# A delta-rule attention feeding an exact-GELU feed-forward on one core: head's copies on ScalarE, weight decoding reordered, one weight load, one solve and one Gram product moved

## The chip, the core and the metric

The program runs on one core of a Trainium2 chip. The metric is the device time of one launch in microseconds. It has five engines with a queue each: TensorE (PE, its weight loads PEld), VectorE (DVE), ScalarE (ACT), GpSimd (POOL) and SyncE (SP), which here issues almost all DMAs.

## The reference

q, k and v are (4, 8, 768, 48): four sequences, eight heads, 768 tokens, head size 48.

```python
k_n = k / (norm(k, axis=-1) + 1e-06)
for t in range(S):
    y[:, :, t] = einsum('bhd,bhde->bhe', q[:, :, t], state)
    v_old = einsum('bhde,bhd->bhe', state, k_n[:, :, t])
    state = state + beta[:, :, t] * einsum('bhd,bhe->bhde', k_n[:, :, t], v[:, :, t] - v_old)
x = y.transpose(0, 2, 1, 3).reshape(B * S, H * D)      # (3072, 384)
h = x @ w_in                                           # w_in (384, 2048)
out = (0.5 * h * (1 + erf(h / sqrt(2)))) @ w_out       # w_out (2048, 384)
```

All is fp32. The words of `w_in` and `w_out` reach the kernel as 64-bit floating numbers, two 32-bit words each, and the kernel makes fp32 of them itself.

## The kernel before, in words

The 768 tokens are cut into 12 chunks of 64; a chunk has two units (`a` = 0, 1), each of two sequences side by side on 128 partitions. For a chunk the recurrence becomes a triangular system of its 64 tokens: Gram products of the keys (`grams`, L419, matmuls psG at L414 and copies at L425), an elimination of its diagonal 32x32 blocks on VectorE for two chunks together (L496 to L503, the transposes back at L512 and L516), and two joining products (psJ; L548 with copies L559 and L563 for the first pair of chunks, L593 later). Then come the products with the running state (`against_state`, psK L667), the right side W (`subtract`, L678 and L684, with y copied at L679), the solution U (`solve`, psU L702, copied by `solved` at L710 and L712), the reading and the change of state (`use`, psY L732, and `update`, L743), the add into the state St (`next_state`, L748), the copy of the reading into x (`read`, L756 or L758), and its transpose xT (`turn`, psX L776 or L779, copied at L780). xT is the input of the feed-forward of that chunk.

The feed-forward of chunks 0 and 1 is plain: `fc1` makes 16 groups of 128 hidden units (psH, L811: three matmuls of 256 columns, six records in the trace, then a GELU on ScalarE, at L902 for chunk 0 and at L817 for chunk 1), `fc2` multiplies them with `w_out` (psO, L829, each product two records, copied at L833). psH and psO share a tag with two buffers, so group f + 2 needs the GELU of group f. From chunk 2 on the two layers use a scheme with fewer products (L916 and L859), which needs sums of weights made beforehand (`sum_of_w_in`, `sum_of_w`).

The weights are decoded in 16 parts: parts 0 to 7 are `w_in` (each serves two groups of fc1), 8 to 15 are `w_out` (`n_in` is 8). A part n passes through `fetch` (L202, DMAs at L213, into four slots for `w_in`, into three for `w_out`), `begin` (the exponent bits, DVE, L231 or L234), `exponents` (ScalarE, L237, or L902 where it is kept in program order), `mantissas` (DVE, L251 and L253) and `signed` (DVE, L260 and L261, after which the slot is fetched anew: part n + 4, or n + 3 for `w_out`). `two_kinks(n)` (L218) picks between two ways: one activation on ScalarE and L260 on DVE, or two activations on ScalarE and no L260. In the kernel before, parts 3 to 7, 9, 10, 12 and 14 use two.

Order. The head is written by hand: everything between L1075 and L1172 keeps its program order on all five engines. After it, VectorE alone keeps the order that `emit` makes: a plan of steps with due times (L1195 and after), sorted by these, in units where the fc1 and fc2 of chunk c lie between about c + 1 and c + 2. The other engines are arranged by the framework's scheduler from the same order, save that `keep` (L901) holds an instruction of ScalarE to its place, and that `together` and `behind` chain products of TensorE. `decode_in` (L278) holds the due times of parts 3 to 7. `load` (L100) fetches keys and queries of a chunk, `load_v` its values, `load_blocks` (L138) the keys or queries of later chunks in sixteen small DMAs. `late` (L1177) closes the pools of the head and opens others in their place.

The part written by hand ends with: decoding of parts 0 to 2, `solve`, `use`, `read`, `turn` and `update` of chunk 0, and its `next_state`. Chunk 1 follows in the plan, between the groups of the first fc1.

Of the kernel before, what the change touches and what calls it, by code (L numbers as in the profile page):

```python
# [19 lines left out]
def kernel(  # L20
# [28 lines left out]
    nc = tc.nc  # L49
# [6 lines left out]
    NA = B // 2  # L56
# [38 lines left out]
    tiles = {}  # L95
# [7 lines left out]
    for c in range(NC):  # L103
        for a in range(NA):
            u = tiles[c, a] = Unit()
# [48 lines left out]
    first = [tiles[c, a] for c in range(2) for a in range(NA)]  # L154
# [38 lines left out]
    n_in = len(w_parts)  # L193
# [23 lines left out]

    def two_kinks(n):  # L218

        return 2 < n < n_in or n > n_in and n % 2 == 0 or n == n_in + 1  # L220

    def high(e, dt):

# [2 lines left out]
    def begin(n):  # L226
        e = su.tile([128, WG], U32, tag="w_e", name="w_e")
        raw = w_raw.pop(n)
        halves[n] = w_parts[n][0].rearrange("q m n -> q (m n)"), raw[:, :, 0], raw[:, :, 1], e
        if two_kinks(n):  # L230
            nc.vector.tensor_scalar(e.bitcast(I32), raw[:, :, 1].bitcast(I32), 20, -1,  # L231
                                    op0=ALU.arith_shift_right, op1=ALU.bitwise_and)
        else:
            nc.vector.tensor_scalar(e, raw[:, :, 1], 20, 0x7FF, op0=ALU.logical_shift_right,  # L234
                                    op1=ALU.bitwise_and)

    def exponents(n, put=lambda fn, *args, **kw: fn(*args, **kw)):  # L237
        e = halves[n][3]
        if two_kinks(n):
            f = e.bitcast(F32)  # L240
            put(nc.scalar.activation, f, e.bitcast(I32), ACT.Prelu, bias=lim[:, 2:3], scale=1.0,
                alpha=FLAT)
            put(nc.scalar.activation, high(e, I16), f, ACT.Prelu, bias=lim[:, 3:4], scale=128.0,
                alpha=1.0 / FLAT)
        else:
            put(nc.scalar.activation, e, e, ACT.Relu, bias=lim[:, 0:1], scale=float(2 ** 23))

    def mantissas(n):
        dst, lo, hi, e = halves[n]
        bits = dst.bitcast(U32)  # L250
        nc.vector.tensor_scalar(bits, hi, 0xFFFFF, 0x100000, op0=ALU.bitwise_and,  # L251
                                op1=ALU.bitwise_or)
        nc.vector.scalar_tensor_tensor(dst, lo, 2.0 ** -32, bits, ALU.mult, ALU.add)  # L253

    def signed(n):

        dst, lo, hi, e = halves.pop(n)
        scale = high(e, BF16) if two_kinks(n) else e.bitcast(F32)
        if not two_kinks(n):
            nc.vector.scalar_tensor_tensor(e, hi, 0x80000000, e, ALU.bitwise_and, ALU.bitwise_or)  # L260
        nc.vector.scalar_tensor_tensor(dst, dst, 2.0 ** -20, scale, ALU.mult, ALU.mult)  # L261
        after = n + (NS if n < n_in else len(slots))
        if (after < n_in) == (n < n_in):
            fetch(after)
# [426 lines left out]
    def solve(us, copies=(nc.scalar.copy, nc.scalar.copy)):  # L691
        psU = dn("psU")
        for u in us:
            zf = Zf[(u.c // 2) % 2]
            if u.c == 0 and u.a:
                psU = dn("psU")
            u.psU = quarters(psU[:, :, u.a * NP * D:(u.a + 1) * NP * D])
            for k in range(NP // 2):
                for r in range(2):
                    for p, s in SIDES:  # L700
                        h = 4 * k + 2 * s + r
                        nc.tensor.matmul(u.psU[HALF[p ^ s], s, k, r, :],  # L702
                                         lhsT=zf[HALF[p], u.t * H + h, :],
                                         rhs=u.W[HALF[p], h, :], start=True, stop=True)
        for u, copy in zip(us, copies):
            solved(u, copy)
# [10 lines left out]
    def use(us):  # L717

        for u in us:
            if u.c == 0 and u.a == 0:  # L720
                u.psY = [ps.tile([128, NP * D], F32, tag="mlp", name="psY").rearrange(
                    "q (k r d) -> q k r d", r=2, d=D) for s in range(2)]
            else:
                psY = dn("psY")
                both = quarters(psY[:, :, 0:NP * D])
                u.psY = [both[:, s] for s in range(2)]
                u.psS = psY[:, :, NP * D:2 * NP * D].rearrange("q p (j d) -> q p j d", d=D)
            for k in range(NP // 2):
                for r in range(2):
                    for p, s in SIDES:  # L730
                        h = 4 * k + 2 * s + r
                        nc.tensor.matmul(u.psY[s][HALF[p ^ s], k, r, :], lhsT=u.P[HALF[p], h, :],  # L732
                                         rhs=u.U[HALF[p], h, :], start=True, stop=True)
            if u.c > 0:
                update(u)

    def update(u):
        if u.c == 0 and u.a == 0:
            u.psS = dn("psS")[:, :, 0:NP * D].rearrange("q p (j d) -> q p j d", d=D)
        if u.c < NC - 1:  # L740
            for j in range(NP):
                for r, p in QUADS:
                    nc.tensor.matmul(u.psS[HALF[r], p ^ r, j, :], lhsT=u.Kp[HALF[p], 2 * j + r, :],  # L743
                                     rhs=u.U[HALF[p], 2 * j + r, :], start=True, stop=True)

    def next_state(u):
        if u.c < NC - 1:
            nc.vector.tensor_tensor(St[:, u.a], St[:, u.a], u.psS, op=ALU.add)  # L748

    def read(u, copy=nc.scalar.copy):  # L750
        u.x = wk.tile([128, H, D], F32, tag="x", name="x")
        both = slice(0, 128)
        for to, at_, s in ((both, both, 0), (HALF[0], HALF[1], 1), (HALF[1], HALF[0], 1)):
            dst, src = pairs(u.x[to], s), u.psY[s][at_]
            if u.c < 2:
                copy(dst, src)  # L756
            else:
                nc.vector.tensor_tensor(dst, src, pairs(u.y[at_], s), op=ALU.add)  # L758
# [7 lines left out]
    def turn(u):  # L766
        if u.a == 0:
            xTs[u.c] = wk.tile([128, NM, NA * 128], F32, tag="xT", name="xT")
        xT = xTs[u.c]
        psX = sq("psX", NM, 128)  # L770
        for m in range(NM):
            cols = slice(m * 128, (m + 1) * 128)
            if u.c == 1:

                for i, part in enumerate((u.x, u.y)):
                    nc.tensor.matmul(psX[:, m, :], lhsT=part.rearrange("q h d -> q (h d)")[:, cols],  # L776
                                     rhs=ident, start=i == 0, stop=i == 1)
            else:
                nc.tensor.transpose(psX[:, m, :], u.x.rearrange("q h d -> q (h d)")[:, cols], ident)  # L779
        nc.scalar.copy(xT[:, :, u.a * 128:(u.a + 1) * 128], psX)  # L780
# [273 lines left out]
    def at(first, last, steps):  # L1054

        total, done, timed = sum(s[0] for s in steps), 0.0, []
        for w, *step in steps:
            timed.append((first + (last - first) * (done + 0.5 * w) / total, step))
            done += w
        return timed  # L1060
# [90 lines left out]
    exponents(0)  # L1151
    mantissas(0)
    begin(1)
    solve(first[:NA], (nc.scalar.copy, nc.vector.tensor_copy))
    exponents(1)
    use(first[:NA])
    read(first[0])
    read(first[1], nc.vector.tensor_copy)
    signed(0)
    mantissas(1)  # L1160
    for u in first[:NA]:
        turn(u)
        update(u)
    signed(1)
    begin(2)
    exponents(2)
    mantissas(2)
    signed(2)
    begin(3)
    for u in first[:NA]:  # L1170
        next_state(u)
    by_hand.close()  # L1172
    free.append(True)
    tc.no_sync_barrier()
# [13 lines left out]
    def state_at(c, *times, first=(), second=()):  # L1188

        steps = state_steps(c, first, second)  # L1190
        if len(times) > len(steps):
# [3 lines left out]
    plan = [at(c + 1 + 0.25 * (c == 1), c + 2 + 0.25 * (c == 0), ffn_steps(c)) for c in range(NC)]  # L1195
    plan += [decode_in(), at(1.365, 1.9, decode_steps(n_in, NW)), at(1.91, 1.911, [(1.0, late)])]
    rows1, join1 = eliminate_steps(1), join_steps(1)
    plan += [at(0.98, 0.985, [(1.0, load, 3)]),
             [(t, (join, 0, range(NA, 2 * NA), level)) for level, t in enumerate((1.085, 1.16))],
]  # L1200
    sums = [(1.0, sum_of_squares, tiles[3, a], h) for a in range(NA) for h in range(H)]
    plan += [at(1.48, 1.8, sums), at(1.81, 1.811, [(1.0, fn, c) for c in (2, 3) for fn in (norms, prep)]), at(1.9, 1.905, [(1.0, finish_both)]), at(2.725, 2.726, [(1.0, queries, third)]),
             at(1.31, 1.311, [(1.0, together, (against_state, first[NA:]))]),
             at(1.361, 1.362, [(1.0, subtract, first[NA:])]),
             at(1.4, 1.401, [(1.0, together, (solve, first[NA:], ()))]),
             at(1.43, 1.431, [(1.0, solved, first[NA], kept_copy)]),
             at(1.455, 1.456, [(1.0, solved, first[NA + 1], kept_copy)]),
             state_at(1, None, None, 1.5, 1.56, 1.58),
# [7 lines left out]
             at(2.7, 2.701, [(1.0, together, join1[1]), (0.0, copy_out, "join", 4)]),  # L1216
             at(2.75, 2.751, [(1.0, together, join1[2]), (0.0, copy_out, "join", 4)]),
             state_at(2, None, 2.772, 2.851, 2.906, 2.922),
             at(2.728, 2.729, [(1.0, norms, 4), (1.0, prep, 4)]), at(2.8, 2.9, [(1.0, grams, [tiles[4, a] for a in range(NA)])])]
    plan += [at(0.995, 1.0, [(1.0, load_v, 2)]), at(2.727, 2.728, [(1.0, sum_of_w, 1, 2)]), at(2.96, 2.961, [(1.0, last_sum_of_w)]), at(3.07, 3.071, [(1.0, sum_of_w, 4)])]  # L1220
    plan += [at(c + 0.958, c + 0.959, [(1.0, mix_x, c)]) for c in range(2, NC)]
    plan += [at(c - 0.4, c - 0.3, v_steps(c)) for c in range(4, NC)]
    plan += [at(2.08, 2.44, [(1.0, scale_head, tiles[c, a], h)
# [110 lines left out]
```

## Time and profile before

| | |
|---|---|
| median of three runs | 646.69 us (646.2 to 648.64) |
| profiled execution | 647.7 us, span 645.9 us |
| TensorE matmuls, busy | 619.9 us (96% of the span), 9702 records |
| TensorE weight loads, busy | 574.0 us |
| VectorE, busy | 496.5 us, 1016 instructions |
| ScalarE, busy | 259.2 us, 581 instructions |
| GpSimd, busy | 62.2 us |
| mean granted TensorE clock | 0.987 |

How to read it: the profile is one execution, and times in it count from its first instruction. An engine's busy share is a mean over stages with different limits; a stage is read from the timeline of its window, where a bracket gives the idle time ahead of an instruction and what ended it. The ends of matmuls are modelled, so two that follow each other overlap on paper; the distance of their starts is the better measure. In the names, `w_e` is the exponent tile of a part, `w_raw` and `w_out_sb` as a source hold undecoded words, `G` holds hidden units, or Gram blocks where its source is psG.

### The profile page before, as it was taken

The numbers are of one execution on the slowest core, as the hardware profiler recorded it, in microseconds if no ns is written. First come the engines' busy times: TensorE is split into PE (matmuls) and PEld (weight loads), VectorE is DVE, ScalarE is ACT, GpSimd is POOL, SyncE is SP. The second block draws the span as 40 slices with busy tenths as digits, with TensorE's granted clock in tenths as the row PEclk, the third lists the DMA queues.
The fourth block names the chain that finished last, engine by engine and source line by source line (L and its number), as shares of the span: only waits on it lengthen the run. The fifth ranks groups of instructions, "written<-read, shape, count | busy, mean of one in ns | idle before, by whom it ended". The sixth has DMA issues, their size and how long they took to land.

```text
span 645.9 us, 22148 instructions
## 1 busy us (share of the span) xinstructions
PE 619.9 (96%) x9702; PEld 574.0 (89%) x9702; DVE 496.5 (77%) x1016; ACT 259.2 (40%) x581; POOL 62.2 (10%) x58
## 2 busy tenths in 40 slices
PE   6769989999999999999999999999999999999997
PEld 5657767776699999999999999999999999999997
DVE  6998789997899997999677999677999564354342
ACT  3574777624452157033157132156132253132230
POOL 4043001100221004001004001004001000000000
PEclk9986999999999999999999999999999999999999
DMA  9794755202433235321325312402212400100101
GB/s 131 174 275 131 155 140 166 37 14 45 80 57 49 56 41 92 52 35 31 68 32 89 59 26 34 73 16 40 50 24 36 69 3 3 25 2 2 26 3 24
DMA packets 158433, 39.79 MB, mean 62 GB/s; under 512 B 150016, under 2 KB 153216, under 8 KB 158336
## 3 DMA queue, kind: packets, MB, share of 16 engines
q1 hardware_dynamic: 155344, 36.94, 29.4%
q10 hardware_dynamic: 2992, 1.43, 1.0%
q8 instruction: 76, 1.25, 0.8%
q14 instruction: 21, 0.17, 0.1%
HBM read 33.62 MB, written 4.72 MB: 59 GB/s over the span
## 4 chain that ended last, share of the span: by engine, by line
PE 83%; DVE 7%; ACT 3%; DMA 3%; issue 2%; SPq 2%; ACTq 0%; DVEq 0%
PE psX L859 12%; PE psY L916 11%; PE psX L916 8%; PE psY L859 8%; PE psV L916 5%; PE psZ L916 5%; PE psO L829 5%; PE psZ L859 4%; PE psG L414 4%; PE psV L859 4%; PE psH L811 3%; PE psK L667 3%; PE psJ L593 2%; PE psY L732 2%; PE psU L702 2%
## 5 line engine op out<-in xcount | busy, mean ns | idle before, releaser
L916 PE MATMUL psX<-xT,w_in_sb 128*128 128x128 f32 x480 | 64.6, 278 | 0.3 <-DVE p L1013 0.2
L503 DVE TENSOR_TENSOR Nu<-Nu,tmp 128x58 f32<-128x58 f32 (+13 forms) x168 | 59.1, 352 | 5.8
L501 DVE TENSOR_TENSOR tmp<-Nu 128x58 f32<-128x58 f32 (+13 forms) x168 | 58.2, 346 | 4.4
L916 PEld LDWEIGHTS psX<-xT,w_in_sb 128*128 128x128 f32 x480 | 58.8, 192 | 1.6 <-issue 0.4
L902 ACT COPY xT<-psX 128x768 f32<-128x768 f32 x9 | 7.2, 798 | 124.4 <-PE psX L788 124.4
L859 PE MATMUL psX<-w_out_sb,G 128*128 128x192 f32 x320 | 55.3, 326 | 0.0
L351 POOL TENSOR_TENSOR n<-n,half 128x16 f32<-128x16 f32 x10 | 29.0, 2903 | 258.0 <-DVE n L349 195.1
L859 PEld LDWEIGHTS psX<-w_out_sb,G 128*128 128x128 f32 x320 | 52.1, 190 | 0.0
L811 PE MATMUL psH<-xT,w_in_sb 128*128 128x256 f32 x192 | 46.0, 396 | 2.4 <-ACT G L902 2.3
L811 PEld LDWEIGHTS psH<-xT,w_in_sb 128*128 128x128 f32 x192 | 37.1, 197 | 9.8 <-ACT G L902 3.9
L829 PE MATMUL psO<-w_out_sb,G 128*128 128x384 f32 x128 | 44.3, 492 | 0.0
L916 PE MATMUL psY<-xT,w_in_sb 128*128 128x128 f32 x320 | 42.3, 275 | 0.0
L902 ACT COPY pu<-psZ 128x512 f32<-128x512 f32 x40 | 23.4, 586 | 39.2 <-PE psZ L916 39.2
L916 PEld LDWEIGHTS psY<-xT,w_in_sb 128*128 128x128 f32 x320 | 38.9, 192 | 0.0
L829 PEld LDWEIGHTS psO<-w_out_sb,G 128*128 128x128 f32 x128 | 23.5, 190 | 13.8
L902 ACT ACTIVATE G<-G 128x512 f32<-128x512 f32 x40 | 25.2, 629 | 19.9 <-DVE G L947 19.2
L376 POOL TENSOR_TENSOR V<-V,n 128x384 f32<-128x384 f32 x18 | 15.7, 882 | 134.0 <-DMA V<-in_v_dram 94.0
L859 PE MATMUL psY<-T,G 128*128 128x192 f32 x160 | 28.6, 332 | 0.0
L859 PE MATMUL psZ<-T,pu 128*128 128x192 f32 x160 | 28.6, 332 | 0.0
L939 DVE TENSOR_TENSOR psY<-psY,pu 128x512 f32<-128x512 f32 x20 | 14.0, 698 | 18.5 <-PE psY L916 18.3
L859 PE MATMUL psV<-w_out_sb,G 128*128 128x192 f32 x160 | 27.7, 326 | 0.0
L859 PE MATMUL psX<-T,G 128*128 128x192 f32 x160 | 27.6, 326 | 0.0
(186 smaller groups left out, 1347.2 us busy)
## 6 DMA issues: line engine op xcount, KB each, us to landing
Kp<-in_k_dram SPq DMA_DIRECT2D x76, 96.0 KB, 3.3
w_out_sb<-in_moe_w_in_dram SPq DMA_DIRECT2D x24, 256.0 KB, 4.5
w_raw<-in_moe_w_out_dram SPq DMA_DIRECT2D x16, 384.0 KB, 4.9
V<-in_v_dram SPq DMA_DIRECT2D x48, 96.0 KB, 3.1
out_dram<-o_sb SPq DMA_DIRECT2D x36, 96.0 KB, 2.2
Qp<-in_q_dram SPq DMA_DIRECT2D x64, 32.0 KB, 2.2
Qp<-in_q_dram SPq DMA_DIRECT2D x16, 96.0 KB, 4.2
Qp<-in_k_dram SPq DMA_DIRECT2D x32, 32.0 KB, 2.4
```

What stands on the lines that cost most here:

```text
L351: nc.gpsimd.tensor_tensor(flat, flat, half, op=ALU.pow)
L376: engine.tensor_tensor(u.V, u.V, ns[u.c][:, u.a].unsqueeze(2).to_broadcast([128, H, D]), op=ALU.mult)
L414: nc.tensor.matmul(psG[HALF[p], r, i * NP + j, :], lhsT=u.Kt[rows, p, j, :], rhs=(u.Qt if x else u.Kt)[rows, p, j, :], start=True, stop=True)
L501: nc.vector.tensor_tensor(tmp, nu[:, j + 1:, j:j + 1].to_broadcast([128, n, j]), nu[:, j:j + 1, 0:j].to_broadcast([128, n, j]), op=ALU.mult)
L503: nc.vector.tensor_tensor(nu[:, j + 1:, 0:j], nu[:, j + 1:, 0:j], tmp, op=ALU.add)
L667: nc.tensor.matmul(u.psK[to, x, r, j, :], lhsT=(u.Qt if x else u.Kt)[rows, p, j, :], rhs=St[rows, u.a, p ^ r, j, :], start=True, stop=True)
L811: nc.tensor.matmul(psH, lhsT=w_in_sb[:, f // 2, m, f % 2 * 128:(f % 2 + 1) * 128], rhs=xTs[c][:, m, :], start=(m == 0), stop=(m == NM - 1))
L829: nc.tensor.matmul(u.psO, lhsT=G[:, u.a, f, :], rhs=w_out_sb[:, f, :], start=(f == 0), stop=(f == NF - 1))
L859: nc.tensor.matmul(ps_, lhsT=lhs[:, f, :], rhs=rhs[:, f, :], start=first and f == 0, stop=f == FH - 1, skip_group_check=not first)
L902: i = fn(*args, **kw)
L916: nc.tensor.matmul(ps_[:, i], lhsT=lhs[:, f // 2, f % 2 * 128:(f % 2 + 1) * 128], rhs=rhs, start=first and i == 0, stop=True, skip_group_c ...
L939: nc.vector.tensor_tensor(L1["Y1"], L1["Y1"], L1["pu"][:, 0], op=ALU.add)
```

## The change

1. `two_kinks`: parts 3 to 7 as before, but of `w_out` now 12, 13 and 14 use two activations (before 9, 10, 12 and 14).
2. In the part written by hand, the copies of the second unit's U and x go from VectorE to ScalarE; `mantissas` of parts 1 and 2 and `signed(0)` come earlier on VectorE; `exponents(1)` and `exponents(2)` come after the first and the second unit's turn on ScalarE; `next_state` of both units comes before `signed(2)` and `begin(3)`.
3. The loads of chunk 3's keys and queries and of chunk 2's values are due later (1.06 and 1.07 in place of 0.98 and 0.995). On SyncE's queue the load of part 7, the eighth group of `w_in`, then comes ahead of them, save for two key loads; the loads after them change places too (the sixteen small loads of chunk 4's key blocks now come before the first loads of `w_out`'s fourth and later parts and chunk 3's values).
4. Chunk 1's right side W (`subtract`) comes earlier on VectorE, ahead of `signed(7)`, its solution U (`solve`) later on TensorE, behind one more group of fc1.
5. The Gram product of chunk 4 is due at 3.045 in place of 2.8 to 2.9: on TensorE it goes from ahead of chunk 2's reading to behind its turns and the first two products of chunk 2's feed-forward, its four copies on ScalarE with it. The last of chunk 1's fc2 and parts of the following transposes change places by a few products.

```diff
     def two_kinks(n):
-        return 2 < n < n_in or n > n_in and n % 2 == 0 or n == n_in + 1
+        return 2 < n < n_in or n_in + 3 < n < n_in + 7
...
     begin(1)
-    solve(first[:NA], (nc.scalar.copy, nc.vector.tensor_copy))
+    mantissas(1)
+    solve(first[:NA])
+    use(first[:NA])
+    for u in first[:NA]:
+        read(u)
+    signed(0)
+    begin(2)
+    mantissas(2)
+    turn(first[0])
+    update(first[0])
     exponents(1)
-    use(first[:NA])
-    read(first[0])
-    read(first[1], nc.vector.tensor_copy)
-    signed(0)
-    mantissas(1)
+    turn(first[1])
+    update(first[1])
+    exponents(2)
+    signed(1)
     for u in first[:NA]:
-        turn(u)
-        update(u)
-    signed(1)
-    begin(2)
-    exponents(2)
-    mantissas(2)
+        next_state(u)
     signed(2)
     begin(3)
-    for u in first[:NA]:
-        next_state(u)
...
-    plan += [at(0.98, 0.985, [(1.0, load, 3)]),
+    plan += [at(1.06, 1.065, [(1.0, load, 3)]),
...
-             at(1.361, 1.362, [(1.0, subtract, first[NA:])]),
-             at(1.4, 1.401, [(1.0, together, (solve, first[NA:], ()))]),
+             at(1.325, 1.326, [(1.0, subtract, first[NA:])]),
+             at(1.42, 1.421, [(1.0, together, (solve, first[NA:], ()))]),
...
-             at(2.8, 2.9, [(1.0, grams, [tiles[4, a] for a in range(NA)])])]
-    plan += [at(0.995, 1.0, [(1.0, load_v, 2)]),
+             at(3.045, 3.046, [(1.0, together, (grams, [tiles[4, a] for a in range(NA)]))])]
+    plan += [at(1.07, 1.071, [(1.0, load_v, 2)]),
```

## The prediction

> **What bounds the kernel now.** First the busy time by stage (columns: stage, length, then busy us and instructions of PE, PEld, DVE, ACT and POOL, granted PE clock, DMA share, GB/s).
>
> ```profile
> 56.26:93.24 36.98, 32.06 (x549) 26.05 (x545) 31.57 (x46) 23.70 (x42) 0.00 (x0) 0.95 0.64 165
> ...
> 99.24:645.90 546.66, 541.02 (x8094) 509.21 (x8092) 412.28 (x848) 199.40 (x434) 41.89 (x26) 1.00 0.24 42
> ```
>
> From 99.24 on PE is busy for 541.02 of 546.66 us: there only PE's own work, or a new wait of PE, counts. From 56.26 to 93.24 no engine is full (PE 32.06, DVE 31.57, ACT 23.70 of 36.98 us), so a ring of waits sets the pace. How much can be had: a group of fc1 (six records) takes 1.295 us (further on in the chain, 24 records take 5.18). After 60.80 PE has 14 groups (18.1), two joins (1.1 each), psK (2.0), psU (1.1) and the reading and state products (2.0): 25.4 us. Without a wait it would end at 86.2; it ends at 93.2. So 7.0 us of waits is the ceiling here.
>
> The chain of waits (start, length, what) names the ring:
>
> ```profile
> 73.51 5.24 DMA w_out_sb<-in_moe_w_in_dram
> ...
> 88.28 1.15 ACT w_e L237
> ...
> 99.40 7.74 PE psO L829 x24
> ```
>
> A part of `w_in` is late, then exponents and GELUs alternate on ScalarE, then PE alone runs. Four timelines show why, a fence each for VectorE, ScalarE, PE and SyncE's queue (start, length, instruction; in the bracket the idle time ahead of it and what ended it):
>
> ```profile
> 52.63 1.09 DVE L756 COPY x<-psY 128x192 f32<-128x192 f32 x3 [1.18 <-PE psY L732]
> 53.76 0.96 DVE L260 SCALAR_TENSOR_TENSOR w_e<-w_out_sb,w_e 128x768 uint32<-128x768 uint32 x1
> ...
> 78.88 0.56 DVE L231 TENSOR_SCALAR w_e<-w_out_sb 128x768 int32<-128x768 int32 x1 [2.76 <-DMA w_out_sb<-in_moe_w_in_dram]
> ```
> ```profile
> 59.54 0.94 ACT L237 ACTIVATE w_e<-w_e,lim 128x768 uint32<-128x768 uint32 x1 [3.73 <-DVE w_e L234]
> 60.39 0.36 ACT L902 ACTIVATE G<-psH 128x256 f32<-128x256 f32 x1
> 63.34 2.13 ACT L902 ACTIVATE w_e<-w_e,lim 128x768 f32<-128x768 int32 x2 [2.59 <-DVE w_e L231]
> ```
> ```profile
> 63.82 1.20 PE L548 MATMUL psJ<-XM,G 32*32 32x32 f32 x64 [1.46 <-DVE St L748]
> ...
> 89.71 1.56 PE L811 MATMUL psH<-xT,w_in_sb 128*128 128x256 f32 x6 [1.28 <-ACT G L902]
> ```
> ```profile
> 69.69 2.65 SPq L100 DMA_DIRECT2D V<-in_v_dram  x4
> 72.43 1.51 SPq L213 DMA_DIRECT2D w_out_sb<-in_moe_w_in_dram  x3
> ```
>
> VectorE leaves decoding at 50.06 for the copies of the second U (from 50.33) and of the second x (52.63), and is back at 53.76: 2.2 us of copies and 1.4 of waits for PE. Later it stands 2.76 us for part 7, whose load SyncE issues at 72.43 behind the loads of chunk 3 and V. ScalarE stands 3.73 and 2.59 us in front of exponents that VectorE has not begun, with finished groups behind them; PE waits for GELUs (1.28) and for the state's add (1.46).
>
> **What the Trainium skill says.** "TensorE: Matmul & The Clock Gate", in the section on the array's architectural detail, says that ScalarE and VectorE are strict FIFOs: the trace agrees (the GELU at 60.39 runs only after exponents that began at 59.54). The same page, Part 1, says that PE runs at half clock until a window of about 3.4 us was busy: the clock is 0.50 from 44 to 60 us, and fc1 starts at 56.26, 3.8 us before it doubles. "ScalarE: Activation LUTs", What ACT_TABLE_LOAD costs, gives 280 ns + 0.833 ns an element with a pointer bias, 0.92 us for 768; the trace has 0.94. "VectorE: DVE Perf Modes", the tier table, gives one-source fp32 operations twice the rate of two-tensor ones: 0.55 against 0.96 us here.
>
> **Copies and order in the head.** ScalarE copies the second U right after the first (0.97 us: 50.47 to 51.45), in the place of `exponents(1)` (50.49 to 51.43), so x of the first unit starts at 51.46 as before; x of the second follows at 52.6, when psY is ready, as it did on VectorE. xT still ends at 55.8 and fc1 starts at 56.26: cost 0, and 1.0 if that cover is gone. PE's clock history is the same. VectorE runs on at 50.06: `mantissas(1)` 1.47, `signed(0)` 1.87 (to 53.4, before 55.7), part 2's 1.94, `signed(1)` when `exponents(1)` is ready at 55.1 (to 57.2), the two state adds 0.93 (58.1, before 64.1), `signed(2)` to 60.0 and part 3's begin there, before at 62.75. So the exponents of part 3 start on ScalarE at 60.5, not 63.34: 2.84 us. The join goes directly behind the third group (1.46 of wait gone); next late is the fourth group, behind those exponents: 63.1, before 65.74.
>
> **Part 7's load.** SyncE issues it when VectorE has read part 3, at 61.9. The old load took until 78.75, 6.3 after its first issue; so it lands by 68.5 and is needed at 73. VectorE's 2.76 us go. What waits behind: chunk 3's loads and V(2), each 1.5 us later, read first at 93.95 (squares) and 115 (scaling): no cost. The sixteen block loads (9 us on the queue, 70 to 79) now precede `w_out`'s part 11, which VectorE releases only at 82: 3 us of cover; V(3) behind them comes near 86 and is scaled from about 118.
>
> **Kinks.** Part 9 has one activation less: ScalarE saves 2.12 - 0.94 = 1.18 us between two GELUs that PE waits for. Part 10 saves the same ahead of chunk 1's x copies; 13 pays it later, beside psO. VectorE gets L260 twice more (0.96 each) by 93 and once less later: net 0.96.
>
> **W and U of chunk 1.** The same instructions, moved. W's four (1.9 us) go ahead of `signed(7)`, so y is copied before the GELUs of f10 and f11; psU goes behind f13, filling PE while ScalarE catches up. I take 0 by itself, between -1 and +1.
>
> **The head's sum.** 2.84 + 2.76 + 1.18 = 6.8 us on ScalarE's chain. To see whether PE lets it through, I walked the order of all three engines with these durations (activations 1.06 each, a GELU 0.33 to 0.36, the decoding of a part 2.4 to 3.9 on VectorE, 0.1 to 0.2 from an end to a waiting start): ScalarE runs exponents 3 from 60.5, 4 from 63.35, copies Zf at 67.0, exponents 5 from 68.65, 6 from 71.45, 7 from 74.35 (VectorE begins part 7 at 73.2), y at 76.6, part 8 at 79.25, part 9 at 81.2, the two U from 82.5 to 84.9. PE then starts the fourth group at 63.1, the ninth at 71.2, psK at 73.8, ends f13 at 81.0, psU at 82.1, f15 at 84.7 and the reading at 86.6, nearly the ceiling's 86.2. I take 87.0: 6.2 before 93.2. Then x (before at 94.17) is copied from 86.7, since part 10 holds it less: PE's wait of 0.39 there goes, and 0.5 is added: 6.7.
>
> **Is it kept?** Decoding has a lead of 6.0 at part 8's begin (84.74 before, 78.7), less 0.96 for L260: 5.1 at its end (114.2, so 109.1). Part 11 is signed at 96.9 and PE wants it at 97.5: just in time. Behind the decoding, on ScalarE, are the clearing of Kb and V's scaling (114.39 to 118.83), ahead of the GELU at 118.83. That GELU frees a buffer at 119.2 for the group that PE starts at 119.9: 0.7 us to spare. Now 12 scalings stand ahead of it, not 15 (0.23 each): 0.7 more. Lead wanted 6.7, covered 5.1 + 0.7 + 0.7: 0.2 to 0.3 lost. Elimination starts 5.1 earlier, with 3.8 us idle before its joins: kept. 6.4.
>
> **Gram 4.** Now its evacuation stands before psY (waits of 0.27 on it, and 0.97 that no semaphore explains, at 164 to 167). Behind the turns, PE reaches the turn up to 2.8 us earlier by its own order and then waits for VectorE's x, at 167.1: most of the gain goes there. Its four copies (0.58 + 0.59 + 1.25 = 2.42) now stand on ScalarE before Qt's copies, which PE needs for chunk 5's Gram: -1.0 to +1.3; I take +0.3, since PE has a product of the layer between.
>
> **Total.** 6.4 + 0.3 = 6.7. The profiled execution is 647.7 (645.9 and 1.8 around it), so 641.0 as such; it lies 1.0 over the median, and the same difference from 646.69 gives 640.0.
>
> **Rivals.** (a) The lead is eaten by decoding: parts 11 and 12 come later than PE wants, or ScalarE's ring is slower than walked, each GELU adding 0.1 to 0.2. For it: 0.6 us of margin at part 11, and ScalarE without slack from 68 to 77. Against: part 12 has 4 us. Price 2.6: 642.6. (b) The head gains little: the serial copies cost their 1.0, the ring's end is PE's own order, so that only part 7's 2.76 count, and Gram 4's copies take 0.5: 1.3 to 2, about 645.0. Against: the 2.84 follow from VectorE's stop, in the trace. (c) Slower: the clock. PE's new short waits at 62.8 and 70.7 fall in the windows after 60, and the full clock isn't granted until psO. The 14 groups at half rate cost 18.1 more, of which 0.8 fit into waits: 640.0 + 17.3 = 657.3. It decides from eight groups on (10.4 us, more than 6.7 + 3.2). Against it:
>
> ```profile
> 58.00:60.00 2.00, 2.00 (x6) 1.55 (x6) 1.94 (x4) 0.46 (x1) 0.00 (x0) 0.50 0.59 175
> 60.00:62.00 2.00, 2.00 (x11) 1.60 (x9) 1.95 (x3) 0.75 (x2) 0.00 (x0) 0.98 0.82 284
> ```
>
> after this grant PE stood for over 2 us between 62 and 66, and the clock stayed 1.00.
>
> **Chances.** Forecast 0.62, (a) 0.20, (b) 0.13, (c) 0.05. A measurement of this kernel can tell 0.5% from no change (3.2 us: 643.5 and 649.9). Faster is the forecast and (a), 0.82; same (b), 0.13; slower (c), 0.05. Range: below, PE at its floor (0.8), Gram 4's better end (1.0) and the 0.3 not lost, 637.9; above, (a) and the copies' lost microsecond, 643.6. About 0.2 is left out: (b), (c) and a few hundredths below.
>
> **What would show it.** VectorE without copies from psU or psY and without a stop before 60; begin of part 3 at 60; the third group's join near 62; part 7's DMA issued near 62 and no wait for it; reading done at 87 (93.2); elimination's start at 109 (114.2); PE full from 92 on. Wrong if fc1 starts after 57, if a GELU wait of over 1 us stays between 66 and 86, if PE waits for `w_out` near 97 or for Qt near 170, or if the clock stays at 0.50 past 62.

## The result, and the profile after

The changed kernel takes 643.72 us (median of eight runs, 641.74 to 645.56); the kernel before took 646.84 in the same series. The ratio is 0.995, with an interval of 0.993 to 0.9969. The gain is 3.1 us; 6.7 were forecast. The profiled execution took 644.36 us with a span of 642.6, against 647.7 and 645.9 before.

By stage, first the head from fc1's start to the end of chunk 1's reading, then all from the third psO on (columns as in the prediction):

```profile
55.78:89.63 33.85, 31.66 (x549) 26.47 (x545) 29.07 (x43) 22.51 (x43) 0.00 (x0) 0.93 0.70 163
94.99:642.60 547.61, 541.32 (x8094) 508.77 (x8092) 413.27 (x850) 200.08 (x436) 42.09 (x26) 1.00 0.24 43
```

The head lasts 33.85 us, before 36.98: 3.1 of the gain lies here, where the prediction had 6.2. Behind it TensorE has the same 541 us of work, in 547.6 us where it had 546.7: 0.9 is given back. The third psO starts 4.25 us earlier than before (0.48 of this is an earlier start of fc1).

The chain of waits (start, length, what) has lost the exponents and has a new long piece of PE:

```profile
63.70 4.54 PE psH L811 x12
...
95.15 7.74 PE psO L829 x24
```

Timelines of the changed kernel (start, length, instruction, and in the bracket the idle time ahead of it), a fence each for VectorE, ScalarE, PE and SyncE's queue:

```profile
49.40 1.19 DVE L251 TENSOR_SCALAR w_in_sb<-w_out_sb 128x768 uint32<-128x768 uint32 x1
50.62 1.47 DVE L253 SCALAR_TENSOR_TENSOR w_in_sb<-w_out_sb,w_in_sb 128x768 f32<-128x768 uint32 x1
...
60.72 0.55 DVE L231 TENSOR_SCALAR w_e<-w_out_sb 128x768 int32<-128x768 int32 x1
...
73.33 0.96 DVE L261 SCALAR_TENSOR_TENSOR w_in_sb<-w_in_sb,w_e 128x768 f32<-128x768 f32 x1 [2.60 <-ACT w_e L902]
...
75.70 0.57 DVE L231 TENSOR_SCALAR w_e<-w_out_sb 128x768 int32<-128x768 int32 x1
```
```profile
61.31 2.13 ACT L902 ACTIVATE w_e<-w_e,lim 128x768 f32<-128x768 int32 x2 [2.97 <-DVE w_e L231]
63.31 0.61 ACT L902 ACTIVATE G<-psH 128x256 f32<-128x256 f32 x2
```
```profile
60.43 1.20 PE L548 MATMUL psJ<-XM,G 32*32 32x32 f32 x64
63.70 4.54 PE L811 MATMUL psH<-xT,w_in_sb 128*128 128x256 f32 x12 [2.07 <-ACT G L902]
```
```profile
62.76 1.86 SPq L213 DMA_DIRECT2D w_out_sb<-in_moe_w_in_dram  x3
```

VectorE makes no copies from psU or psY, and part 3 begins at 60.72 (before 62.75, predicted 60.0). Part 7's load is issued at 62.76 (before 72.43), and the wait for it is gone; part 7 begins at 75.70. But two things are new. The first steps of part 1 take 1.19 and 1.47 us where the same steps of part 2 take 0.55 and 0.96. And PE, which in the kernel before stood 1.46 us ahead of the join and 0.72 behind it, now stands 2.07 us in one piece; the two groups after that take 4.54 us, not 2.86. The windows of two microseconds show why (the third figure from the end is the granted clock):

```profile
60.00:62.00 2.00, 1.63 (x67) 1.19 (x65) 1.97 (x4) 0.69 (x1) 0.00 (x0) 1.00 0.75 243
62.00:64.00 2.00, 0.29 (x1) 0.30 (x2) 1.74 (x3) 1.97 (x5) 0.00 (x0) 0.95 0.99 294
64.00:66.00 2.00, 2.00 (x6) 1.54 (x6) 1.91 (x4) 1.90 (x2) 0.00 (x0) 0.50 1.02 260
```

PE is idle for most of 62 to 64, and the clock falls to half (at 63.80) just as its work returns.

### The profile page after: what moved, and what is told of

The parts are those of the page before. It is cut to its first block, busy times and chain, and to the rows that moved or that the text cites. A ratio compares the mean times of both kernels' runs of the same rounds, so it can differ in the third digit from the quotient of the medians.

```text
span 642.6 us, 22154 instructions
## 1 busy us (share of the span) xinstructions
PE 621.4 (97%) x9702; PEld 575.8 (90%) x9702; DVE 496.1 (77%) x1011; ACT 259.7 (40%) x586; POOL 63.7 (10%) x58
## 4 chain that ended last, share of the span: by engine, by line
PE 86%; DVE 6%; ACT 3%; DMA 2%; issue 1%; SPq 1%; DVEq 0%; ACTq 0%
PE psX L859 12%; PE psY L916 11%; PE psX L916 8%; PE psY L859 8%; PE psH L811 6%; PE psV L916 5%; PE psO L829 5%; PE psZ L916 5%; PE psG L414 4%; PE psZ L859 4%; PE psV L859 4%; PE psK L667 3%; PE psJ L593 2%; PE psY L732 2%; PE psU L702 2%; DMA Kp<-in_k_dram 1%
```

## The experiments

Three series of four kernels. In each the kernel before was run beside them (its median: 647.24, 647.26 and 646.50 us), so ratios to it are compared, and 0.001 is 0.65 us. In the expectations, "the GELU of the fourth group" is that of the second group (f1): it frees the buffer that the fourth one waits for.

**The GELU ahead of the exponents of part 3.**

```diff
-        marks = {3: (None, 1.03, 0.99, 1.04), ...
+        marks = {3: (None, 1.05, 0.99, 1.055), ...
```

> The changed kernel with one order on ScalarE turned round: the GELU of the fourth group of chunk 0 (f1 of the second unit's pair) goes ahead of the exponents of part 3. Theory 1 (the clock): in the changed kernel PE stood 2.07 us for this GELU behind those exponents, and the granted clock then fell to 0.50 from 63.9 to 67.1; the two groups there took 4.48 us, not 2.6. It expects no PE wait over 1 us there, the clock at 1.00 from about 60 on, and 1.5 to 2.5 us off the changed kernel's time: 641.2 to 642.2. Rival (VectorE is late anyway): the join and the next GELU then wait for part 3's exponents, which begin only at 61.3; the reading ends at the same 89.6, and the time stays at 643.7 within 0.5.

Measured: 641.26 us, ratio 0.9913 [0.9895, 0.9931], 2.4 us less than the changed kernel. PE (its timeline) runs on behind the join and has a pause of 1.36 us instead of 2.07:

```profile
60.98 1.56 PE L811 MATMUL psH<-xT,w_in_sb 128*128 128x256 f32 x6
63.91 1.56 PE L811 MATMUL psH<-xT,w_in_sb 128*128 128x256 f32 x6 [1.36 <-ACT G L902]
```

The clock stays at 1.00 in every window from 56 on, and the reading ends at 87.6. The first theory's time holds, though a pause of over 1 us was left. But two things changed at once, the order and the clock.

**V's scaling later.** GpSimd's two scalings of V of chunk 1 (one for each of its units) ran at 49.13 to 51.27, beside part 1's steps.

```diff
-    for u in first[NA:]:
-        scale_v(u)
...
     begin(3)
+    nv = wk.tile([128, NA, H], F32, tag="nv", name="nv", bufs=1)
+    nc.vector.tensor_copy(nv, n0[:, NA:])
+    ns[1] = nv
+    for u in first[NA:]:
+        scale_v(u)
```

> The changed kernel with GpSimd's two scalings of V of the first chunk held back until VectorE has begun part 3 (they read a copy of the scale that VectorE makes then; one small VectorE copy is added). Theory 2 (GpSimd beside VectorE): the first steps of part 1 took 1.19 and 1.47 us on VectorE, while the same steps take 0.55 and 0.96 elsewhere, because GpSimd scaled V at the same time. It expects 0.55 and 0.96 there, part 3's begin at about 59.7 instead of 60.72, and through it an earlier GELU, so that PE's wait at 61.6 falls from 2.07 to about 1.0 us and the clock may stay: 1.0 us off (642.7) without the clock's part, 2.5 us (641.2) with it. Rival: GpSimd's work now slows the steps around 61 to 63 by the same 1.1 us, and the time stays at 643.7 within 0.5.

Measured: 643.88 us, 0.9937 [0.9919, 0.9955]. VectorE's timeline:

```profile
49.85 0.55 DVE L251 TENSOR_SCALAR w_in_sb<-w_out_sb 128x768 uint32<-128x768 uint32 x1
50.44 0.96 DVE L253 SCALAR_TENSOR_TENSOR w_in_sb<-w_out_sb,w_in_sb 128x768 f32<-128x768 uint32 x1
...
61.14 1.47 DVE L253 SCALAR_TENSOR_TENSOR w_in_sb<-w_out_sb,w_in_sb 128x768 f32<-128x768 uint32 x1
62.53 1.18 DVE L231 TENSOR_SCALAR w_e<-w_out_sb 128x768 int32<-128x768 int32 x1
```

The delay goes from part 1 and turns up in the same size where GpSimd works now: it is GpSimd's scaling that costs VectorE 0.5 to 0.6 us at each of two steps. The time gains nothing that can be told: PE came to the join sooner still (59.27 against 60.43), stood 2.53 us for the GELU, and the clock fell as in the changed kernel.

**Gram 4 back in its place.**

```diff
-             ... at(3.045, 3.046, [(1.0, together, (grams, [tiles[4, a] for a in range(NA)]))])]
+             ... at(2.8, 2.9, [(1.0, grams, [tiles[4, a] for a in range(NA)])])]
```

> The changed kernel with the Gram of chunk 4 put back to its place ahead of the last turns. Theory 3: in the changed kernel the lead of 4.25 us at the third psO shrinks to 3.3 by chunk 3's psK, since the four copies of this Gram stand ahead of Qt on ScalarE and PE then waits 1.00 us for Qt; back in its place it gives 0.5 to 1.0 us less: 642.7 to 643.2. The prediction's own figure was that the move gains 0.3, so 644.0.

Measured: 644.8 us, 0.9959 [0.9944, 0.9975]. My third theory falls: put back, the Gram product costs something (0.6 us by the ratios, within their intervals) and gains nothing. In its trace PE waits 0.27, 1.53 and 0.34 us at this place, 2.14 in all; in the changed kernel 0.49, 0.62 and 1.00, 2.11 in all.

**The kinks back.**

```diff
-        return 2 < n < n_in or n_in + 3 < n < n_in + 7
+        return 2 < n < n_in or n > n_in and n % 2 == 0 or n == n_in + 1
```

> The changed kernel with the two-kink forms of the parts as they were before (part 9 with one activation more on ScalarE and one VectorE operation less). The prediction priced it at 1.18 us in ScalarE's chain: 644.9. Rival: with the waits and the clock of the changed kernel the end of the head is set by PE's order and not by ScalarE's chain at part 9: 643.7 within 0.4.

Measured: 644.44 us, 0.995 [0.9931, 0.9969], as the changed kernel. The rival holds, but a second cover had to be excluded (below).

**PE kept busy in the pause, first attempt.**

```diff
+        again = 3 if (g, level, ts[0]) == (0, 0, NA) else 1
-        for i, u in enumerate(range(ts[0] * H, (ts[-1] + 1) * H)):
+        for i, u in list(enumerate(range(ts[0] * H, (ts[-1] + 1) * H))) * again:
```

> The changed kernel, with PE's products of the first join of the second unit's pair written three times instead of once (the same values into the same place, 1.1 us each): PE is busy in the 2.07 us in which it waited for the GELU, and nothing else changes place. Clock theory: the wait itself switched the clock to 0.50. It expects the clock at 1.00 from 58 to 70, the two groups at 63.7 in 2.6 us instead of 4.48, the reading done near 87.8 instead of 89.6, and a time of 641.8 to 642.3. Rival (the clock falls for another reason, or VectorE and ScalarE set the end of the head whatever PE's speed is): the clock still falls or the end of the head stays at 89.6, and the time stays at 643.7 to 644.0.

Measured: 646.91 us, 0.9983 [0.9969, 0.9997]. It didn't do what it was made for. PE's timeline:

```profile
61.17 3.06 PE L549 MATMUL psJ<-XM,G 32*32 32x32 f32 x181
66.37 0.52 PE L549 MATMUL psJ<-XM,G 32*32 32x32 f32 x11 [2.14 <-issue]
```

After 181 of the 192 products PE stood 2.14 us for nothing that the profile names, and everything behind came later. The clock fell here too, at 65.03, when that wait (from 64.23) was 0.8 us old and PE had been busy with the join's products until then. So the run doesn't test the theory as it was meant to, but it shows that the length of the pause is not what the clock goes by (below).

**PE kept busy, second attempt.** The third group's six products are written twice, ahead of the join.

```diff
-        for m in range(NM):
+        for m in list(range(NM)) * (1 + (c == 0 and f == 2)):
```

> The changed kernel, with the six products of the third group of fc1 (chunk 0) written twice into the same place: 1.3 us of full-size work for PE directly ahead of the join, in a stretch where PE then waits 2.07 us for a GELU. Nothing after the join is due earlier than before (the third group's own GELU runs only at 63.6). The fourth group still starts at 63.7, and PE's pause is about 0.8 us. Clock theory (a pause of about 2 us switches the clock to half): the clock stays at 1.00, the two groups take 2.6 us instead of 4.48, and the time falls by up to 1.9 us, to 641.8 to 642.6 (ratio to before 0.992 to 0.9935), though PE does more. Rival: the clock falls all the same or the time stays at 643.7 within 0.5 (ratio 0.994 to 0.996), and the speed of PE in the two groups was hidden behind VectorE and ScalarE.

Measured: 642.16 us, 0.9932 [0.992, 0.9944]. With 1.3 us more to do PE is faster. Its timeline, and the windows with the clock:

```profile
62.31 1.20 PE L548 MATMUL psJ<-XM,G 32*32 32x32 f32 x64
64.17 2.86 PE L811 MATMUL psH<-xT,w_in_sb 128*128 128x256 f32 x12 [0.67 <-ACT G L902]
```
```profile
64.00:66.00 2.00, 1.83 (x8) 1.63 (x9) 1.94 (x3) 1.97 (x4) 0.00 (x0) 1.00 1.08 249
```

Here the order on ScalarE is that of the changed kernel, the fourth group starts even later (64.17 against 63.70), and the two groups take 2.86 us instead of 4.54, since the clock stayed. The reading ends 1.2 us earlier (88.4 against 89.6): 1.7 for the clock, less 0.5 for the later start. By the ratios it is 1.2 us; the two intervals overlap, so it is the trace that carries this. It separates the clock from the order.

**The loads back.**

```diff
-    plan += [at(1.06, 1.065, [(1.0, load, 3)]),
+    plan += [at(0.98, 0.985, [(1.0, load, 3)]),
...
-    plan += [at(1.07, 1.071, [(1.0, load_v, 2)]), ...
+    plan += [at(0.995, 1.0, [(1.0, load_v, 2)]), ...
```

> The changed kernel with the load of chunk 3 and the second load of V back ahead of part 7's load. The prediction's term: part 7 then comes 2.76 us late on VectorE. In the changed kernel VectorE begins part 7 at 75.70 and the old load landed at 78.75 in the kernel before (it is issued there 1 us or so earlier here, since VectorE reads part 3 sooner): a wait of 2 to 3 us and a time of 645.5 to 646.5. Rival: with the GELU's wait and the clock in front, half of it is hidden: 644.3 to 645.

Measured: 645.64 us, 0.9972 [0.9959, 0.9984]: 1.4 us more than the changed kernel by the ratios, just over the rival's 0.6 to 1.3 and under the term's 1.8 to 2.8. VectorE's wait for part 7 is only 0.59 us, behind one of 3.55 for exponents that the longer fall of the clock (62.5 to 69.3) had delayed. That fall was twice as long as in the changed kernel's trace, so the 1.4 us need not be the load's alone.

**W and U of chunk 1 back.**

```diff
-             at(1.325, 1.326, [(1.0, subtract, first[NA:])]),
-             at(1.42, 1.421, [(1.0, together, (solve, first[NA:], ()))]),
+             at(1.361, 1.362, [(1.0, subtract, first[NA:])]),
+             at(1.4, 1.401, [(1.0, together, (solve, first[NA:], ()))]),
```

> The changed kernel with W and U of chunk 1 back in their places of before. The prediction took 0 for this move, between -1 and +1: 643.7. Rival, the move is what lets PE run from 79 to 87 without a wait: PE then waits for GELUs of f10 to f13 about 0.5 to 1.3 us and the time is 644.3 to 645.

Measured: 645.95 us, 0.9977 [0.9968, 0.9986]: 1.7 us more. PE waits 0.55 us at 82 for a GELU and 0.65 at 90 for the copy of U, of the rival's kind, though at U and not only at GELUs, and more than its 0.6 to 1.3. These waits make 1.2 of the 1.7 us.

**The head's order alone, on the kernel before.** The edit is the hand-written part of the change and nothing else of it.

```diff
-    solve(first[:NA], (nc.scalar.copy, nc.vector.tensor_copy))
+    mantissas(1)
+    solve(first[:NA])
...
+    signed(2)
+    begin(3)
```

> The kernel before, with only the hand-written order of the head (copies on ScalarE, exponents, sums of the state) as in the changed kernel; loads, kinks, W and U and Gram 4 as before. The prediction's term for this part is 2.84 us: 644.0. What the other runs show would give less: the GELU behind the exponents of part 3 makes PE pause over 2 us and halves the clock, VectorE loses 1.1 us beside GpSimd, and part 7's load comes when it came, so that the gain is 0 to 1 us: 646 to 647 (ratio 0.9985 to 1.0).

Measured: 646.58 us, 0.9998 [0.9987, 1.0009]: no gain. PE (timeline) stands 3.00 us for the GELU, the clock falls from 65 to 68, and later the second activation of part 9 stands in front of a GELU again:

```profile
64.10 4.54 PE L811 MATMUL psH<-xT,w_in_sb 128*128 128x256 f32 x12 [3.00 <-ACT G L902]
...
88.29 1.56 PE L811 MATMUL psH<-xT,w_in_sb 128*128 128x256 f32 x6 [1.27 <-ACT G L902]
```

VectorE waits 1.28 us for part 7, which begins at 77.47.

**A version without both faults.** The GELU first, and V's scaling held back to the join's two steps on VectorE, which read PSUM.

```diff
-        marks = {3: (None, 1.03, 0.99, 1.04), ...
+        marks = {3: (None, 1.05, 0.99, 1.055), ...
...
+        if (g, level, ts[0]) == (0, 0, NA):
+            nc.vector.tensor_copy(nv, n0[:, NA:])
+            ns[1] = nv
+            for u in first[NA:]:
+                scale_v(u)
...
-    for u in first[NA:]:
-        scale_v(u)
...
+    nv = wk.tile([128, NA, H], F32, tag="nv", name="nv", bufs=1)
```

> The changed kernel with the fourth group's GELU ahead of the exponents of part 3, and GpSimd's two scalings of V held back until VectorE starts its join copies, which read PSUM (they read a copy of the scale made then; one small VectorE copy is added). If GpSimd slows VectorE only where VectorE works on SBUF alone, the steps of part 1 are back at 0.55 and 0.96, the join's two at 1.41 for both, and the time is 0.5 to 1.1 us below the version with the GELU's order alone (ratio to before 0.9896 to 0.9905 instead of 0.9913). Rival: PE's later waits for GELUs and the clock take the microsecond up, and it stays within 0.3 us of that version; a loss would mean that GpSimd slows the steps after the join.

Measured: 640.84 us, 0.9902 [0.9887, 0.9918]: the fastest, 3.1 us below the changed kernel, and 6.3 below the kernel before. Part 1's steps are back at 0.55 and 0.96. GpSimd's scaling and VectorE's join (timelines) lie side by side, and neither is slower for it:

```profile
63.69 1.41 DVE L564 TENSOR_TENSOR XM<-psJ,gm 32x512 f32<-32x512 f32 x2
```
```profile
63.74 1.62 POOL L376 TENSOR_TENSOR V<-V,nv 128x384 f32<-128x384 f32 x2 [11.20 <-DVE nv L553]
```

Against the version with the GELU's order alone the gain is 0.7 us by the ratios, within their intervals. From fc1's start to the end of the reading both take the same (31.75 and 31.82 us), so what VectorE won is not seen in PE's end.

**That version with the loads back, and with the kinks back.** The edits are those above.

> The fastest version so far (the changed kernel with the fourth group's GELU first and V's scaling held back) with the load of chunk 3 and the second load of V back ahead of part 7's load. With the changed kernel itself this cost about 1.4 us, and VectorE's wait for part 7 was 0.59. If the load's term of 2.76 was right where nothing else delays ScalarE, it costs 2 to 3 us here: ratio 0.9935 to 0.995. If the load is late by its landing time alone, PE's ring has slack there and it costs about 1.4 again or less: 0.991 to 0.9925.

Measured: 645.47 us, 0.9981 [0.9965, 0.9997]: 5.1 us more, outside both expectations. VectorE and PE (timelines):

```profile
78.12 0.56 DVE L231 TENSOR_SCALAR w_e<-w_out_sb 128x768 int32<-128x768 int32 x1 [4.82 <-DMA w_out_sb<-in_moe_w_in_dram]
```
```profile
82.92 4.40 PE L816 MATMUL psH<-xT,w_in_sb 128*128 128x256 f32 x12 [4.15 <-ACT G L907]
```

The load comes when it came in every kernel with the old order (part 7 begins at 78.88, 77.54, 77.47 and 78.12 there), so the earlier VectorE is, the longer it waits. PE's pause is 4.15 us, and the clock falls at 82.66. The fourteen times lie in two groups, six from 643.24 to 644.06 and eight from 645.12 to 648.35; the trace is one of the eight (647.55), so the 5.1 us are a mixture, and what the trace shows need not hold for the six.

> The fastest version so far with the two-kink forms as they were before. In the changed kernel this made no difference that could be measured (0.995 for both), where the prediction had 1.18 us. If the 1.18 us were only covered by the clock's fall there, they show here: ratio 0.9915 to 0.9925. Rival: PE sets the end of the head by its own order, and the ratio stays at 0.9895 to 0.991.

Measured: 641.04 us, 0.9909 [0.9895, 0.9923]: 0.5 us more by the ratios, not told apart from none. What its trace shows is PE's wait of 0.40 us for x, which the change had removed.

## Why the prediction was wrong

Its mechanism was right in the main (VectorE without copies, part 7 in time), its size was not: 3.1 us where it had 6.7. Two terms failed in the head: the clock, put at nothing (1.7 us), and VectorE's durations (1.1 us). Point by point.

- **Copies on ScalarE, cost 0: right.** fc1 starts at 55.78 (before 56.26).
- **"So the exponents of part 3 start on ScalarE at 60.5": 0.8 too early.** They start at 61.31. VectorE was full as forecast, but GpSimd's scaling took 0.64 and 0.51 us from it. In the kernel before, VectorE copied from PSUM in that stretch, and the cost was not there to be read. Durations were taken from steps that ran with GpSimd at rest. The Trainium skill, "SBUF — State Buffer", section "SBUF: two separate sides", says that VectorE and GpSimd share a pair of ports as an exclusive lock, which a VectorE operation in a two-port mode takes, or one with two SBUF inputs against a GpSimd operation that reads SBUF. The trace agrees in kind (0.55 to 1.19, 0.96 to 1.47, and 1.41 unchanged for the join, whose source is in PSUM).
- **"After this grant PE stood for over 2 us between 62 and 66, and the clock stayed 1.00": the step that failed.** The reading of that trace is true (waits of 1.46 and 0.72 us with a join between them), but rival (c), the clock, was dismissed on it as if it held for every execution and every order. In the changed kernel's trace the wait is one of 2.07 behind the join, the clock fell, and (c) came in a small form, for two groups and not fourteen: 1.7 us (4.54 against 2.86). That two waits became one is not what decided, as is worked out below.
- **"PE's clock history is the same": wrong too.** The clock rose at 57.0, before at 60.1; in the other twelve traces it rose between 51.5 and 58.4. Traces with the same hand-written head differ in it too (55.65 to 57.98 with the loads, the kinks or the Gram back), so it can't be carried from one trace to the next. Here the early rise made fc1's first groups faster, and PE stood longer for the same GELU.
- **The sum of 6.2 in the head.** Measured from fc1's start, the fourth group begins after 7.92 us, where the prediction had 6.84: 1.1 for VectorE's lost time. The clock takes 1.7. The remaining 0.3 is not traced. Without both faults the head gets shorter by 5.2 (31.75 against 36.96), and the whole kernel by 6.3: nearly the forecast. But it is not the forecast's sum: the kinks gave at most 0.5 of their 1.18, W and U gave 1.7 where 0 was said, and the GELU's order is not in the forecast at all. That the totals come so close is in part luck.
- **Part 7's 2.76: the wait was gone, but it was no term of a sum.** Put back, it cost 1.4 us behind the clock's fall, and 5.1 in the mean where nothing else was late. Likewise the head's order alone, with 2.84 in the sum, gave nothing while the load still set the date of part 7. They lie one behind the other on one ring, and each is worth only what the next leaves.
- **Kinks, 1.18: mis-sized.** In both kernels 0 to 0.5. PE's order, not ScalarE, ended the head at part 9; the x copy's 0.40 is what is left.
- **W and U, 0 within 1: too low.** They are worth 1.7 us, 1.2 of it in PE's two waits of 0.55 and 0.65; the rest is not traced. In the changed kernel PE's timeline marks no wait from 69 to 95.
- **"Is it kept?": right.** From the third psO (94.99) to the one at 134.18 the lead falls from 4.25 to 3.84, 0.4 where 0.3 was said, though of a lead of 6.7. In the version with the GELU first, with a lead of 6.29 there, the same 0.4 went. PE doesn't wait for part 11 near 97.
- **Gram 4, +0.3 between -1.0 and +1.3: in its range.** One of the prediction's signs of being wrong did come: PE waits 1.00 us for Qt (174.4 to 175.4). In the changed kernel's own trace the lead falls by 0.9 here, of which 0.4 comes back later. ScalarE (timeline) shows from what:

```profile
168.01 2.46 ACTq L823 DMA_DIRECT2D out_dram<-o_sb  x2
170.59 0.94 ACT L902 ACTIVATE ksq<-Kp 128x384 f32<-128x384 f32 x2 [2.61 <-DMA Kp<-in_k_dram]
```

The issue of two stores took 2.46 us on ScalarE's queue, while SyncE issued loads of keys; ksq, the copies of pu, the Gram's and Qt's stand behind it. (The bracket names a load of keys; that its landing held ksq up, and not the issue that ended 0.1 us before, is not excluded.) In the version with the GELU first the same issue took 1.15 us, PE waited 0.48 and 0.68 us there, and nothing was lost (546.65 us from the third psO on, before 546.66). Why an issue takes twice as long in some executions isn't settled.

How sure is the clock? In all fourteen traces every stretch of full or half clock between 45 and 90 us is a whole multiple of 3.41 us (the changed kernel: full from 56.98 to 63.80, half to 67.22). So the clock is set anew at borders 3.41 us apart, and each trace can be cut into windows at its own borders. These are five of them (columns as above), of the version with the loads back and of join_thrice, where the clock fell at the window's end, and of the kernel before (two) and the version with the GELU first, where it stayed:

```profile
59.07:62.48 3.41, 2.01 (x69) 1.51 (x67) 3.34 (x6) 0.92 (x1) 0.00 (x0) 1.00 0.82 262
```
```profile
61.62:65.03 3.41, 2.61 (x165) 2.50 (x158) 2.91 (x5) 3.29 (x5) 0.00 (x0) 1.00 0.99 287
```
```profile
60.09:63.51 3.42, 2.27 (x10) 1.51 (x9) 3.38 (x5) 0.83 (x3) 0.00 (x0) 1.00 0.61 205
63.51:66.92 3.41, 2.38 (x69) 2.15 (x70) 3.38 (x6) 3.13 (x5) 0.00 (x0) 1.00 0.96 270
```
```profile
62.49:65.90 3.41, 1.79 (x9) 1.19 (x8) 3.08 (x5) 3.38 (x5) 0.00 (x0) 1.00 0.92 247
```

For every kernel, the table has the window that ended in the fall or, where the clock stayed, the one at the pause with the least of fc1; "fc1" is the busy time of fc1's products alone, and "best" is the version without both faults:

```
                 window            fc1, us   PE busy, us   pause, us
the clock fell at the end of the window
changed          60.39 to 63.80    0.21      1.34          2.07
V later          59.16 to 62.57    0.18      1.31          2.53
Gram back        61.39 to 64.81    0.47      1.46          1.97
kinks back       61.20 to 64.61    0.30      1.44          2.41
join thrice      61.62 to 65.03    0.00      2.61          2.14
loads back       59.07 to 62.48    0.88      2.01          2.88
W and U back     62.13 to 65.54    0.99      0.99          3.01
head alone       61.67 to 65.09    0.99      0.99          3.00
best + loads     79.24 to 82.66    0.00      0.00          4.15
the clock stayed
before           63.51 to 66.92    1.18      2.38          1.46
GELU first       62.49 to 65.90    1.62      1.79          1.36
third twice      61.25 to 64.66    1.61      2.75          0.67
best             61.75 to 65.17    1.56      1.82          1.22
best + kinks     65.19 to 68.60    1.56      2.92          0.49
```

The pauses part the two groups as well, at 1.5 to 2 us, but they can't be what the clock goes by: with the loads back it fell 1.4 us into the pause (61.07 to 62.48), in join_thrice 0.8 us into it, and the 1.46 of the kernel before brought no fall. Nor can PE's busy time: 2.61 and 2.01 us fell, 1.79 stayed. What parts them is the time of fc1's 128x128 products in the window: at most 0.99 us where the clock fell, at least 1.18 in every other window that starts at full clock between 55 and 83 us. So the join's 32x32 products count for less, and perhaps for nothing. (Three windows that start between 51.5 and 52.4, nearly all ahead of fc1, kept the clock on 64x64 products and transposes, with PE busy for 2.77 to 2.87 us.)

The Trainium skill, "TensorE: Matmul & The Clock Gate", Part 1, says that an idle window of about 3.4 us is what halves the clock, and that the window runs free of the program. The traces agree with the length and with a window that the program doesn't set (the borders lie elsewhere in each). They don't agree with "idle": in eight of the nine windows that ended in a fall PE was busy for 0.99 to 2.61 us, and the measurement decides.

This changes what the failed step means. The kernel before has no product of fc1 from 62.37 to 65.74, 3.4 us; the changed kernel has none from 60.50 to 63.70, 3.2 us. The stretch was there before the change. In the one trace of the kernel before a border at 63.51 fell into it and left 2.27 and 1.18 us on its two sides; by this account the clock stayed up by luck. An estimate from these figures: a window that may hold 1.0 us of fc1 at most must cover 2.4 of the changed kernel's 3.2 us, which about half of its possible places do. The eight times of the changed kernel do lie in two groups, four from 641.74 to 643.07 and four from 644.36 to 645.56; but only one of them was traced (644.36, with the fall), so that half of its executions keep the clock is not shown. Nor is it shown what such a fall would cost in the kernel before, where VectorE's wait of 2.76 us for part 7 comes after it.

## What to carry to other kernels

When TensorE has waits with only small products between them, count how much full-size work is left in any 3.4 us there, and not only the length of each wait. A clock that stayed up in one trace shows one place of the windows; work that fills the stretch (the GELU first, the third group twice) helps wherever they lie. Gains along one ring of waits aren't added: a load with a fixed arrival turns every other gain into a wait for it. And a duration taken from a stretch where GpSimd rested doesn't hold beside GpSimd's work.

## What the hardware showed that was not expected

- The clock changed only at borders 3.41 us apart. It fell after windows with at most 0.99 us of fc1's 128x128 products, one of them with 2.61 us of 32x32 products, and not after those with 1.18 or more; the loss was 1.7 us in two groups. Six products written for nothing (1.3 us) cost less than the fall.
- GpSimd's 128x384 scalings slowed a VectorE step of one source from 0.55 to 1.19 us and one of two from 0.96 to 1.47; beside VectorE's steps on PSUM (1.41) they cost nothing. GpSimd's clearing of Zf at 46.87 to 49.05 slowed the first of these kinds (0.98), but not the second (0.96).
- 192 products of 32x32 in a row stopped at the 181st for 2.14 us, with no semaphore behind it. One packet of the instruction queue moved at 63 to 64 us, with the DMA engines over 90% busy; that PE waited for its instructions is a guess.
